# Attention followed by a two-layer MLP in split fp16: a planner that knows of the port shared by VectorE and GpSimd, lo halves in two operations, and new tables

## The chip, the core and the metric

The kernel is one program on one core of a Trainium2 chip. The time is that of the device from the program's start to its end, in microseconds (us). Names of engines are those of the profile: PE is TensorE, PEld its weight loads, DVE is VectorE, ACT is ScalarE, POOL is GpSimd, and SP issues the DMAs.

## What is computed

```
scores = q @ k.T / sqrt(64)                    # 4 batches, 12 heads, 448 rows, head size 64
scores = where(upper triangle, -1e9, scores)
attn = softmax(scores)
x = (attn @ v)  -> (4 * 448, 768)
h = x @ w_in                                   # w_in 768 x 2048
g = h - tanh(h)
out = g @ w_out                                # w_out 2048 x 768
```

The two weight matrices arrive as 64-bit floats and are turned into 32-bit ones on the core. q, k and v arrive as 32-bit floats.

## The kernel before

**Precision.** All large products run in fp16 with each operand split in two: hi is the scaled value rounded to fp16, lo is the scaled value minus hi. A product is three matmuls (hi·hi, hi·lo, lo·hi). `split` makes the halves. `scaled` makes hi on DVE, ACT or POOL. The lo half is either one DVE pass (`scalar_tensor_tensor`: multiply, then subtract) or, on POOL, two passes: scale the source in place, then subtract hi.

**Stages.** `w_in_chunk` (8 times) turns 256 columns of w_in into fp32, measures their size with a matmul against ones, and splits them; `w_out_half` (twice) does the same for w_out. `first_rows` computes attention for the first 128 rows of two batches at a time; the first pair of batches makes chunk c, the second pair chunk c2. `attention(b)` computes the other 320 rows of batch b, in six pairs of heads: `prep` splits k, q and v, `weights_unit` and `weights_last` do scores, softmax and the split of the weights, a DMA transposes the weights, and `values` multiplies them with v. `mlp_g` is the first MLP layer for a chunk (16 column blocks of 18 matmuls each, evacuated by a tanh on ACT and a pass on DVE, and then split into g), `mlp2` the second layer, whose result leaves through the tile `o`.

**What sets the order.** Nothing is issued where it is written. Every operation is recorded in `Work` with a rank, and `schedule` then plays a list schedule: each engine takes, of what is ready, the operation of lowest rank, with a cost per operation from `cost`. The instructions are issued in the order that this gives, and each engine keeps that order on the chip. Two tables feed it. `CFG` says for each kind of operation on which engine its instances go in turn (V, A, G for DVE, ACT, POOL): `"p": "VAVV"` puts the hi halves of the softmax weights on DVE, ACT, DVE, DVE and so on. `RANK` sets the ranks of the stages; matmuls of the MLP have a rank of 10 and more, attention(b) for b of 1 and more has `RANK["att"] + 10 + b - 1` plus a sixth per pair.

**The shared port in the plan.** `schedule` keeps a time `port` until which operations marked `shared` of DVE and POOL exclude each other. An operation of POOL is marked when it reads a tile. One of DVE is marked when it reads two large operands from SBUF, or when it is a `tensor_scalar` with one large input, no other input, and equal types of input and output.

Of the kernel before, what the change touches and what calls it, by code (L numbers as in the profile page):

```python
# [15 lines left out]
AF = mybir.ActivationFunctionType  # L16
ALU = mybir.AluOpType
# [8 lines left out]
class Work:  # L26
# [43 lines left out]
    def add(self, eng, method, args, kw):  # L70
# [26 lines left out]
        if eng == "G":  # L97
            shared = bool(ins)
        else:
            two_ports = method == "tensor_scalar" and len(big) == 1 and outs[0].dtype == big[0].dtype and len(ins) == 1  # L100
            shared = eng == "V" and (len(big) > 1 or two_ports)
# [4 lines left out]

    def either(self, tag, *ways):
# [6 lines left out]
        n = self.turn[tag] = self.turn.get(tag, -1) + 1  # L114
        way = CFG[tag]
        self.ops[-1].update(eng=way[n % len(way)], tag=(tag, n))

    def cost(self, eng, method, outs, ins):
# [18 lines left out]
        if eng == "A":  # L137
            return n * 0.833 + (51 if psum else 94) + 93 * aps + 93 * (len(outs) > 1), 0.0
        if eng == "G":
            if method == "tensor_tensor":  # L140
                return n * 1.885 + 148, 0.0
            return n * 0.83 + 245, 0.0
# [16 lines left out]
    def schedule(self):  # L159
        n = len(self.ops)  # L160
# [14 lines left out]
        for _ in range(n):  # L175
# [5 lines left out]
            o = self.ops[i]  # L181
            if e in o["shared"] and port > t:
# [19 lines left out]
            if e in o["shared"]:  # L202
                t = max(t, port)
                port = t + o["cost"]
            o["start"] = t
# [13 lines left out]
            for j in users[i]:  # L219
                left[j] -= 1  # L220
                f = self.ops[j]["eng"]
                at[j] = max(at[j], end + (self.SAME if f == e else self.LAT)[f])
                if not left[j]:
                    heapq.heappush(waiting[f], (at[j], j))
# [34 lines left out]
def attention_then_mlp(ctx, tc, qk, v, w_in, w_out, out):  # L259
# [565 lines left out]

CFG = {"early": 4, "e_bufs": 4, "b_out": "A", "b_qk": "AAV", "shift_in": "AGG", "inverse": "A", "w_in": "AVGA", "w_in_lo": "GGV", "shift_out": "AVAG", "w_out": "VAAA", "w_out_lo": "V", "p0": "G", "p0t": "AVAA", "x0": "VVVAAV", "g0": "GGGA", "g0_lo": "V", "g2": "GVVV", "g2_lo": "G", "g": "VVGV", "g_lo": "G", "o": "V", "k_first": "VAVGGA", "k_first_lo": "VVGV", "q_first": "G", "q_first_lo": "V", "v_first": "GVA", "v_first_lo": "V", "p_first": "AGGAVA", "p_first_lo": "V", "k": "GVGG", "k_lo": "V", "q": "VA", "q_lo": "G", "v": "GVAV", "v_lo": "GVV", "p": "VAVV", "p_lo": "VGV", "x": "AAVA"}
RANK = {"c0": -14.292, "w_in": -12.778, "evac": 4.208, "w_out": 7.476, "c0b": 9.316, "att0": -13.314, "att": -0.165}

# [29 lines left out]
```

## Time and profile before

| what | us |
|---|---|
| median of 3 runs (lowest, highest) | 605.71 (604.11, 606.19) |
| profiled execution, its own time | 603.75 |
| its span, first to last instruction | 602.0 |
| PE busy | 559.2 |
| DVE busy | 451.6 |
| POOL busy | 312.9 |
| ACT busy | 294.8 |

A PE that the profile shows as busy is one with a matmul under way; a matmul of 384 columns is shown for 326 ns, while the next one starts 163 ns later. So waiting of PE is read from gaps, and the pace from the starts. DVE instructions overlap a little in the same way, by some 75 ns. All instructions carry the line of one helper (L232), so groups are told apart by their tiles.

### The profile page before, as it was taken

How to read it: one execution, taken by the hardware profiler on the slowest of the kernel's cores; microseconds unless marked ns; L12 is line 12 of the kernel's file. 1: busy time of each engine (PE TensorE's matmuls, PEld its weight loads, DVE VectorE, ACT ScalarE, POOL GpSimd, SP SyncE). 2: the span in 40 equal slices, each digit the busy share in tenths (PEclk: the TensorE clock that was granted, in tenths of full speed). 3: DMA queues.
4: the chain of work that ended last, by engine and by line, in shares of the span. 5: the costliest groups of instructions: out<-in, count | busy, mean ns of one | idle time of the engine just before them, and what ended most of it. 6: DMA issues, size and time to landing. Idle time of an engine off the chain costs nothing.

```text
span 602.0 us, 13635 instructions
## 1 busy us (share of the span) xinstructions
PE 559.2 (93%) x5144; PEld 375.9 (62%) x5144; DVE 451.6 (75%) x1286; ACT 294.8 (49%) x796; POOL 312.9 (52%) x389
## 2 busy tenths in 40 slices
PE   3688689999999999999999999999999999999997
PEld 3456468876555556765666666665666566776664
DVE  3889997989999999999959999921999961332000
ACT  5899899983366755553436463400644430121000
POOL 3577962883232157886528788510687820465000
PEclk9999899999999999999999999999999999999999
DMA  8995467645386974448563556640334281000100
GB/s 283 327 337 186 141 196 212 188 127 222 95 164 142 181 164 79 80 99 181 119 141 72 106 123 174 128 74 27 84 60 79 42 146 43 13 2 1 27 27 26
DMA packets 113378, 74.02 MB, mean 123 GB/s; under 512 B 89760, under 2 KB 99488, under 8 KB 112800
## 3 DMA queue, kind: packets, MB, share of 16 engines
q1 hardware_dynamic: 113312, 73.15, 48.8%
q8 instruction: 40, 0.66, 0.5%
q14 instruction: 26, 0.21, 0.1%
HBM read 45.61 MB, written 5.51 MB: 85 GB/s over the span
## 4 chain that ended last, share of the span: by engine, by line
PE 31%; DVE 31%; issue 3%; DMA 3%; POOL 3%; ACT 1%; DVEq 0%; SPq 0%; POOLq 0%; ACTq 0%
PE b_m L232 29%; DVE pn L232 6%; DVE prob L232 6%; DVE small L232 5%; DVE first L232 3%; DVE t L232 3%; DVE g L232 2%; PE b_x L232 2%; DVE v L232 2%; DVE k L232 1%; DMA e<-in_v_dram 1%; DVE x L232 1%; DMA slot<-in_qk_dram 1%; POOL g L232 1%; DMA pt<-pn 1%
## 5 line engine op out<-in xcount | busy, mean ns | idle before, releaser
L232 PE MATMUL b_m<-x,w_in 128*128 128x320 f16 (+1 forms) x1728 | 230.1, 291 | 15.3 <-DVE t L232 14.2
L232 PEld LDWEIGHTS <-w_in 128*128 128x128 f16 x1728 | 167.5, 98 | 72.1 <-issue 22.9
L232 PE MATMUL b_m<-slot,g 128*128 128x384 f16 x1152 | 192.4, 326 | 0.0
L232 PEld LDWEIGHTS <-g 128*128 128x128 f16 x1152 | 110.7, 98 | 74.9 <-issue 3.9
L232 ACT ACTIVATE prob<-prob,small 128x256 f32<-128x256 f32 (+2 forms) x102 | 58.8, 577 | 70.0 <-DVE small L232 69.5
L232 POOL TENSOR_SCALAR t<-t,small 128x320 f32<-128x320 f32 (+1 forms) x80 | 53.4, 668 | 51.6 <-DVE g L232 43.9
L232 ACT ACTIVATE t<-b_m,small 128x320 f32<-128x320 f32 (+1 forms) x96 | 48.1, 502 | 63.7 <-PE b_m L232 53.6
L232 DVE SCALAR_TENSOR_TENSOR t<-b_m,small,t 128x320 f32<-128x320 f32 (+1 forms) x96 | 49.9, 520 | 30.2 <-ACT t L232 30.0
L232 DVE TENSOR_SCALAR o<-b_m,small 128x384 f32<-128x384 f32 x28 | 17.1, 610 | 70.3 <-PE b_m L232 70.2
L232 POOL TENSOR_TENSOR g<-t,g 128x320 f16<-128x320 f32 x64 | 54.2, 847 | 5.3
L232 DVE CUSTOM_DVE_ANT_0 prob<-b_s,mask,small 128x384 f32<-128x384 f32 (+1 forms) x87 | 46.1, 545 | 0.2
L232 DVE SCALAR_TENSOR_TENSOR slot<-b_s,e 128x384 int32<-128x384 int32 x64 | 34.6, 547 | 5.5 <-ACT b_s L232 3.2
L232 DVE SCALAR_TENSOR_TENSOR pn<-prob,small,pn 128x256 f16<-128x256 f32 (+2 forms) x60 | 37.5, 645 | 0.1
L232 PEld LDWEIGHTS <-v 128*64 128x64 f16 x1296 | 31.5, 111 | 8.2 <-issue 8.0
L232 PE MATMUL b_m<-slot,first 128*128 128x384 f16 x192 | 33.6, 326 | 0.0
L232 PEld LDWEIGHTS <-first 128*128 128x128 f16 (+2 forms) x282 | 21.7, 98 | 17.6 <-issue 6.2
L232 PE MATMUL b_s<-k,q 64*128 64x256 f16 (+2 forms) x342 | 30.7, 317 | 0.4 <-DVE small L232 0.3
L232 ACT ACTIVATE e<-slot 128x768 f32<-128x768 f32 (+1 forms) x30 | 26.3, 876 | 5.4 <-DMA slot<-in_moe_w_in_dram 3.5
L232 POOL TENSOR_SCALAR prob<-prob,small 128x384 f32<-128x384 f32 (+2 forms) x24 | 15.4, 640 | 24.5 <-DVE pn L232 16.3
L232 DVE TENSOR_SCALAR g<-t,small 128x320 f16<-128x320 f32 x48 | 27.1, 564 | 0.4
L232 PE MATMUL b_x<-pt,v 128*64 128x64 f16 (+1 forms) x1026 | 26.3, 207 | 0.3 <-DMA pt<-pn 0.3
L232 DVE TENSOR_SCALAR small<-small 128x1 f32<-128x1 f32 (+4 forms) x159 | 26.0, 178 | 0.2
(137 smaller groups left out, 815.9 us busy)
## 6 DMA issues: line engine op xcount, KB each, us to landing
slot<-in_moe_w_in_dram SPq DMA_DIRECT2D x16, 768.0 KB, 6.2
slot<-in_qk_dram SPq DMA_DIRECT2D x18, 384.0 KB, 3.3
slot<-in_moe_w_out_dram SPq DMA_DIRECT2D x8, 768.0 KB, 4.7
e<-in_moe_w_out_dram SPq DMA_DIRECT2D x8, 768.0 KB, 4.5
e<-in_v_dram SPq DMA_DIRECT2D x3, 1536.0 KB, 6.6
out_dram<-o SPq DMA_DIRECT2D x24, 192.0 KB, 1.9
first<-in_qk_dram SPq DMA_DIRECT2D x6, 384.0 KB, 3.4
g<-in_qk_dram SPq DMA_DIRECT2D x6, 256.0 KB, 6.5
```

What stands on the lines that cost most here:

```text
L232: getattr(self.eng[o["eng"]], method)(*args, **kw)
```

## The change

The planner: a DVE `tensor_scalar` with one large input counts as shared whenever neither its input nor its output lies in PSUM, whatever the types and the scale operand. That takes in the hi halves, which go from fp32 to fp16 with a scale per row. A shared operation may now start a little ahead of the port's release (`lead`) and holds it a little longer. POOL's two-input cost rises by 20, some ACT costs by 75. An operation of cost zero adds no delay to its user on the same engine.

The lo half: `split` records two operations. The first scales the source in place, on POOL or on ACT, or does nothing when DVE does the lo half in one pass. The second is the DVE pass or POOL's subtraction. The letter A in a lo table now means: ACT scales, POOL subtracts.

The tables: most entries of `CFG` and all of `RANK` are new.

```diff
-            two_ports = method == "tensor_scalar" and len(big) == 1 and outs[0].dtype == big[0].dtype and len(ins) == 1
+            two_ports = method == "tensor_scalar" and len(big) == 1 and not any(x.space == bass.MemoryType.PSUM for x in outs + ins)
...
+    def nothing(self, eng):
+        self.ops[-1]["alts"][eng] = [], [0.0]
+        self.ops[-1].setdefault("shared", set())
...
-            return n * 0.833 + (51 if psum else 94) + 93 * aps + 93 * (len(outs) > 1), 0.0
+            words = ins[0].space != bass.MemoryType.PSUM and (o.space == bass.MemoryType.PSUM or ins[0].ap[-1][0] > 1)
+            return n * 0.833 + (51 if psum else 94) + 93 * aps + 93 * (len(outs) > 1) + 75 * (words and not aps), 0.0
...
+            lead = 190.0 if e == "V" else 135.0
+            if e in o["shared"] and port - lead > t:
...
-                t = max(t, port)
-                port = t + o["cost"]
+                t = max(t, port - lead)
+                port = t + o["cost"] + (75.0 if e == "V" else 22.0)
...
-        def lo_pool():
-            G.tensor_scalar(src, src, s, 1.0, ALU.mult, ALU.mult)
-            G.tensor_tensor(lo, src, hi, ALU.subtract)
-        wk.either(tag + "_lo", lambda: V.scalar_tensor_tensor(lo, src, s, hi, ALU.mult, ALU.subtract), lo_pool)
+        wk.either(tag + "_lo", lambda: wk.nothing("V"), lambda: G.tensor_scalar(src, src, s, 1.0, ALU.mult, ALU.mult),
+                  lambda: A.activation(src, src, AF.Copy, scale=s))
+        wk.either(tag + "_lo", lambda: V.scalar_tensor_tensor(lo, src, s, hi, ALU.mult, ALU.subtract),
+                  lambda: G.tensor_tensor(lo, src, hi, ALU.subtract), again=True, A="G")
...
-RANK = {"c0": -14.292, "w_in": -12.778, "evac": 4.208, "w_out": 7.476, "c0b": 9.316, "att0": -13.314, "att": -0.165}
+RANK = {"c0": -25.732, "w_in": -23.993, "evac": 0.14, "w_out": 7.706, "c0b": -9.849, "att0": -0.222, "att": -8.619}
```

What the new table does to the splits, counted in the two programs. Each cell is the number of instructions on DVE / ACT / POOL; POOL's two passes of a lo half count as two, and an ACT scaling with its POOL subtraction as one on each.

| operation | before | after |
|---|---|---|
| w_in hi | 2 / 4 / 2 | 0 / 0 / 8 |
| w_in lo | 2 / 0 / 12 | 8 / 0 / 0 |
| w_out lo | 16 / 0 / 0 | 12 / 4 / 4 |
| g lo of chunk c | 16 / 0 / 0 | 0 / 0 / 32 |
| softmax weights hi, batches 1 to 3 | 67 / 23 / 0 | 45 / 45 / 0 |
| softmax weights lo, batches 1 to 3 | 60 / 0 / 60 | 23 / 45 / 89 |
| k hi, batches 1 to 3 | 5 / 0 / 13 | 6 / 6 / 6 |
| k lo, batches 1 to 3 | 18 / 0 / 0 | 4 / 5 / 23 |
| q hi, batches 1 to 3 | 9 / 9 / 0 | 18 / 0 / 0 |
| q lo, batches 1 to 3 | 0 / 0 / 36 | 6 / 6 / 18 |
| v hi, batches 1 to 3 | 9 / 4 / 5 | 0 / 13 / 5 |
| v lo, batches 1 to 3 | 12 / 0 / 12 | 0 / 0 / 36 |
| g hi, the last four chunks | 48 / 0 / 16 | 32 / 32 / 0 |
| g lo, the last four chunks | 0 / 0 / 128 | 32 / 0 / 64 |
| o | 28 / 0 / 0 | 7 / 21 / 0 |

The order at three places follows.

POOL while w_in is prepared (slot_69 and slot_70 hold the fp32 chunk, w_in_76 and following its halves, pn_103 softmax rows of `first_rows`, e_74 the low words of the next chunk). Before:

```order
L232 TENSOR_SCALAR slot_69<-slot_69,small_105 128x1536
L232 TENSOR_TENSOR w_in_76<-slot_69,w_in_76 128x1536
L232 TENSOR_SCALAR e_74<-slot_68 128x768
L232 TENSOR_SCALAR slot_70<-slot_70,small_105 128x1536
L232 TENSOR_TENSOR w_in_77<-slot_70,w_in_77 128x1536
L232 TENSOR_TENSOR pn_103<-pn_103,small_105 128x512
```

and now:

```order
L239 TENSOR_SCALAR w_in_76<-slot_69,small_105 128x1536
L239 TENSOR_TENSOR pn_103<-pn_103,small_105 128x512
L239 TENSOR_SCALAR w_in_77<-slot_70,small_105 128x1536
L239 TENSOR_SCALAR e_74<-slot_67 128x768
L239 TENSOR_TENSOR pn_103<-pn_103,small_105 128x512
L239 TENSOR_SCALAR w_in_78<-slot_69,small_105 128x1536
```

The scaling in place and the subtraction of the lo half are gone from POOL, which makes the hi half instead; the lo half is a `SCALAR_TENSOR_TENSOR` of 1536 columns in DVE's queue.

POOL in the attention of a later batch (prob_99 and following hold the softmax rows, pn_103 and first_91 the split weights or k and q, t_86 and following MLP rows, g_84 their split). Before:

```order
L232 TENSOR_SCALAR t_87<-t_87,small_105 128x320
L232 TENSOR_TENSOR g_84<-t_87,g_84 128x320
L232 TENSOR_SCALAR t_88<-t_88,small_105 128x320
L232 TENSOR_TENSOR g_84<-t_88,g_84 128x320
L232 TENSOR_SCALAR prob_99<-prob_99,small_105 128x256
L232 TENSOR_TENSOR pn_103<-prob_99,pn_103 128x256
```

and now:

```order
L239 TENSOR_SCALAR prob_99<-prob_99,small_105 128x256
L239 TENSOR_SCALAR slot_70<-slot_70,small_105 128x448
L239 TENSOR_TENSOR pn_103<-prob_99,pn_103 128x256
L239 TENSOR_TENSOR pn_103<-prob_100,pn_103 128x256
L239 TENSOR_TENSOR pn_103<-prob_102,pn_103 128x384
L239 TENSOR_TENSOR first_91<-slot_70,first_91 128x448
L239 TENSOR_TENSOR first_91<-slot_70,first_91 128x320
```

POOL's queue holds lo halves of softmax weights, k and q where it held those of g; several are subtractions alone, whose scaling stands in ACT's queue.

DVE behind the last split of softmax weights of the last batch (pn_103 written from prob_102 or first_91; x_85 is the attention's result on its way to the MLP, o_89 and o_90 results of the MLP, t and g the evacuation of the MLP's first layer). Before:

```order
L232 TENSOR_SCALAR pn_103<-prob_102,small_105 128x448
L232 SCALAR_TENSOR_TENSOR pn_103<-first_91,small_105,pn_103 128x448
L232 SCALAR_TENSOR_TENSOR x_85<-b_x_110,x_85 128x320
L232 TENSOR_SCALAR o_90<-b_m_112,small_105 128x384
L232 TENSOR_SCALAR x_85<-b_x_110 128x320
L232 SCALAR_TENSOR_TENSOR x_85<-b_x_110,x_85 128x320 x2
L232 TENSOR_SCALAR o_89<-b_m_111,small_105 128x384
L232 TENSOR_SCALAR o_90<-b_m_112,small_105 128x384
L232 SCALAR_TENSOR_TENSOR t_88<-b_m_111,small_105,t_88 128x320
```

and now:

```order
L239 SCALAR_TENSOR_TENSOR pn_103<-prob_102,small_105,pn_103 128x448
L239 TENSOR_SCALAR o_90<-b_m_112,small_105 128x384
L239 TENSOR_SCALAR small_105<-small_105 128x2
L239 COPY small_105<-small_105 64x2
L239 SCALAR_TENSOR_TENSOR t_87<-b_m_111,small_105,t_87 128x320
L239 SCALAR_TENSOR_TENSOR g_84<-t_87,small_105,g_84 128x320
L239 SCALAR_TENSOR_TENSOR t_88<-b_m_112,small_105,t_88 128x320
```

Behind that split stood the evacuations of one chunk's first layer (16 of t), now those of two (32). On PE, behind the last score matmul, stood 288 matmuls of 320 columns and 432 of 384; now 576 and 630, and one more pair's values.

## Rows read from the trace of the kernel before

**Rows 1.** The page's busy times by engine (us, share of the span, instructions), and its 40 slices of 15 us for PE and DVE, each digit a busy share in tenths.

```profile
PE 559.2 (93%) x5144; PEld 375.9 (62%) x5144; DVE 451.6 (75%) x1286; ACT 294.8 (49%) x796; POOL 312.9 (52%) x389
...
PE   3688689999999999999999999999999999999997
...
DVE  3889997989999999999959999921999961332000
```

**Rows 2.** Stretches of 20 us: length, then busy us (and instructions) of PE, PEld, DVE, ACT and POOL, the granted clock, the DMA engines' share and GB/s.

```profile
60.00:80.00 20.00, 12.59 (x106) 9.91 (x104) 18.80 (x66) 17.77 (x41) 15.82 (x13) 0.91 0.44 138
...
80.00:100.00 20.00, 18.89 (x174) 15.43 (x172) 17.52 (x49) 19.67 (x51) 11.40 (x13) 1.00 0.75 213
...
340.00:360.00 20.00, 18.55 (x234) 12.93 (x233) 20.00 (x56) 12.19 (x38) 16.67 (x22) 1.00 0.60 123
...
380.00:400.00 20.00, 20.00 (x170) 12.37 (x168) 11.08 (x27) 4.53 (x13) 7.28 (x9) 1.00 0.78 140
400.00:420.00 20.00, 20.00 (x171) 12.38 (x169) 3.39 (x6) 0.95 (x2) 1.85 (x2) 1.00 0.06 20
...
460.00:480.00 20.00, 18.20 (x133) 11.32 (x131) 19.13 (x48) 9.06 (x26) 15.03 (x19) 1.00 0.28 54
```

**Rows 3.** The same for three longer stretches.

```profile
160.00:500.00 340.00, 331.64 (x3438) 212.78 (x3438) 296.01 (x831) 159.59 (x480) 193.48 (x254) 1.00 0.54 112
106.00:136.00 30.00, 27.97 (x249) 24.19 (x249) 27.77 (x55) 25.37 (x52) 25.39 (x33) 1.00 0.53 156
136.00:160.00 24.00, 23.12 (x148) 14.11 (x147) 22.50 (x39) 8.27 (x14) 6.16 (x9) 1.00 0.47 179
```

**Rows 4.** What PE waited for from 106 us to the end: us in total, times, the longest.

```profile
PE b_m L232 <- DVE t L232: 6.9, 12, 1.0
PE b_s L232 <- DVE small L232: 1.5, 3, 1.0
PE b_scales L232 <- DVE small L232: 1.2, 2, 0.9
```

**Rows 5.** Timeline (start us, us, instructions): PE at two long runs of one shape, and the last lines of the chain that ended last.

```profile
503.55 8.95 PE L232 MATMUL b_m<-slot,g 128*128 128x384 f16 x54
512.33 7.91 PE L232 MATMUL b_m<-x,w_in 128*128 128x320 f16 x57
...
503.62 94.82 PE b_m L232 x630
598.46 0.62 DVE o L232
```

**Rows 6.** Timeline of the preparation of w_in: the size matmuls on PE of the first, the fifth and the last chunk, POOL's lo half of the last chunk, and the first evacuation-bound start of chunk c2.

```profile
19.40 1.46 PE L232 MATMUL b_scales<-w_in,ones 128*128 128x256 bf16 x6
...
49.32 0.82 PE L232 MATMUL b_scales<-w_in,ones 128*128 128x256 bf16 x6
...
72.63 1.48 PE L232 MATMUL b_scales<-w_in,ones 128*128 128x256 bf16 x6
...
79.56 1.57 POOL L232 TENSOR_SCALAR slot<-slot,small 128x1536 f32<-128x1536 f32 x1 [0.46 <-ACT w_in L232]
81.21 3.12 POOL L232 TENSOR_TENSOR w_in<-slot,w_in 128x1536 f16<-128x1536 f32 x1
...
106.21 12.13 PE L232 MATMUL b_m<-x,w_in 128*128 128x256 f16 x108 [0.38 <-DVE t L232]
```

**Rows 7.** The passes that write one tile (duration in ns: least / median / most, first and last start in us, shapes): w_in, softmax weights, k and g.

```profile
L232 DVE SCALAR_TENSOR_TENSOR w_in<-slot,small,w_in x2: 1819/1954/2090, 41.6 to 65.5; 128x1536 f16<-128x1536 f32 x2
L232 DVE TENSOR_SCALAR w_in<-slot,small x2: 1280/1293/1306, 28.5 to 63.8; 128x1536 f16<-128x1536 f32 x2
L232 POOL TENSOR_SCALAR w_in<-slot,small x2: 1547/1548/1548, 40.0 to 69.7; 128x1536 f16<-128x1536 f32 x2
L232 DVE SCALAR_TENSOR_TENSOR pn<-prob,small,pn x60: 461/604/1309, 166.0 to 482.4; 128x256 f16<-128x256 f32 x24, 128x384 f16<-128x384 f32 x24, 128x448 f16<-128x448 f32 x12
L232 DVE TENSOR_SCALAR pn<-prob,small x41: 333/431/1240, 170.3 to 489.2; 128x384 f16<-128x384 f32 x16, 128x256 f16<-128x256 f32 x15, 128x448 f16<-128x448 f32 x10
L232 DVE SCALAR_TENSOR_TENSOR k<-slot,small,k x14: 659/778/1210, 160.4 to 457.8; 128x448 f16<-128x448 f32 x14
L232 DVE SCALAR_TENSOR_TENSOR v<-e,small,v x12: 734/740/1302, 210.1 to 465.8; 128x512 f16<-128x512 f32 x12
L232 POOL TENSOR_TENSOR pn<-prob,pn x15: 669/914/1283, 225.6 to 490.5; 128x256 f16<-128x256 f32 x6, 128x384 f16<-128x384 f32 x6, 128x448 f16<-128x448 f32 x3
L232 DVE TENSOR_SCALAR g<-t,small x48: 371/427/1005, 231.2 to 552.9; 128x320 f16<-128x320 f32 x48
L232 DVE SCALAR_TENSOR_TENSOR g<-t,small,g x16: 457/480/1645, 59.5 to 104.8; 128x256 f16<-128x256 f32 x16
```

**Rows 8.** Timeline of DVE and POOL where a hi half of g on DVE meets a lo half of v on POOL.

```profile
231.17 0.37 DVE L232 TENSOR_SCALAR g<-t,small 128x320 f16<-128x320 f32 x1
...
232.18 1.16 POOL L232 TENSOR_TENSOR v<-e,v 128x512 f16<-128x512 f32 x1
...
232.52 1.00 DVE L232 TENSOR_SCALAR g<-t,small 128x320 f16<-128x320 f32 x1
```

**Rows 9.** Groups of DVE from 160 to 500 us: busy us, mean ns of one, idle us before them.

```profile
L232 DVE TENSOR_SCALAR g<-t,small 128x320 f16<-128x320 f32 x36 | 22.4, 623 | 0.0
```

More of the change, by code (lines that the diff above doesn't have):

```diff
@@ L105, in add, with either @@
         op["move"] += move
-    def either(self, tag, *ways):
+    def either(self, tag, *ways, again=False, A="A"):
         self.ops.append(dict(alts={}, deps=set(), rank=self.rank, move=0.0))
@@ L113, in either @@
         self.alt = None
-        n = self.turn[tag] = self.turn.get(tag, -1) + 1
-        way = CFG[tag]
-        self.ops[-1].update(eng=way[n % len(way)], tag=(tag, n))
+        n = self.turn[tag] = self.turn.get(tag, -1) + (not again)
+        way = CFG[tag].replace("A", A)
+        self.ops[-1].update(eng=way[n % len(way)], tag=(tag, n), A=A)
+    def nothing(self, eng):
+        self.ops[-1]["alts"][eng] = [], [0.0]
+        self.ops[-1].setdefault("shared", set())
     def cost(self, eng, method, outs, ins):
@@ L137, in cost @@
         if eng == "A":
-            return n * 0.833 + (51 if psum else 94) + 93 * aps + 93 * (len(outs) > 1), 0.0
+            words = ins[0].space != bass.MemoryType.PSUM and (o.space == bass.MemoryType.PSUM or ins[0].ap[-1][0] > 1)
+            return n * 0.833 + (51 if psum else 94) + 93 * aps + 93 * (len(outs) > 1) + 75 * (words and not aps), 0.0
         if eng == "G":
             if method == "tensor_tensor":
-                return n * 1.885 + 148, 0.0
+                return n * 1.885 + 168, 0.0
             return n * 0.83 + 245, 0.0
@@ L181, in schedule @@
             o = self.ops[i]
-            if e in o["shared"] and port > t:
+            lead = 190.0 if e == "V" else 135.0
+            if e in o["shared"] and port - lead > t:
                 other = [x for x in ready[e] if e not in self.ops[x[1]]["shared"]]
@@ L221, in schedule @@
                 f = self.ops[j]["eng"]
-                at[j] = max(at[j], end + (self.SAME if f == e else self.LAT)[f])
+                at[j] = max(at[j], end + (self.LAT[f] if f != e else self.SAME[f] if o["cost"] else 0.0))
                 if not left[j]:
@@ L823, in attention_then_mlp @@
         wk.emit()
-CFG = {"early": 4, "e_bufs": 4, "b_out": "A", "b_qk": "AAV", "shift_in": "AGG", "inverse": "A", "w_in": "AVGA", "w_in_lo": "GGV", "shift_out": "AVAG", "w_out": "VAAA", "w_out_lo": "V", "p0": "G", "p0t": "AVAA", "x0": "VVVAAV", "g0": "GGGA", "g0_lo": "V", "g2": "GVVV", "g2_lo": "G", "g": "VVGV", "g_lo": "G", "o": "V", "k_first": "VAVGGA", "k_first_lo": "VVGV", "q_first": "G", "q_first_lo": "V", "v_first": "GVA", "v_first_lo": "V", "p_first": "AGGAVA", "p_first_lo": "V", "k": "GVGG", "k_lo": "V", "q": "VA", "q_lo": "G", "v": "GVAV", "v_lo": "GVV", "p": "VAVV", "p_lo": "VGV", "x": "AAVA"}
-RANK = {"c0": -14.292, "w_in": -12.778, "evac": 4.208, "w_out": 7.476, "c0b": 9.316, "att0": -13.314, "att": -0.165}
+CFG = {"early": 4, "e_bufs": 4, "b_out": "A", "b_qk": "AVA", "shift_in": "VGAGAA", "inverse": "VAVV", "w_in": "G", "w_in_lo": "V", "shift_out": "GAGVVV", "w_out": "GAA", "w_out_lo": "AVVV", "p0": "G", "p0t": "VA", "x0": "A", "g0": "AGGG", "g0_lo": "G", "g2": "AAGG", "g2_lo": "GVG", "g": "AAVV", "g_lo": "VG", "o": "AVAA", "k_first": "AVAA", "k_first_lo": "GV", "q_first": "GVV", "q_first_lo": "VGVA", "v_first": "AAVV", "v_first_lo": "GVAA", "p_first": "GA", "p_first_lo": "V", "k": "GAV", "k_lo": "AGVG", "q": "V", "q_lo": "GGAAVV", "v": "AGAA", "v_lo": "G", "p": "AVVA", "p_lo": "VAGA", "x": "VA"}
+RANK = {"c0": -25.732, "w_in": -23.993, "evac": 0.14, "w_out": 7.706, "c0b": -9.849, "att0": -0.222, "att": -8.619}
 _OUTS = [((1792, 768), "float32")]
```

## The prediction

> **What bounds the kernel now.** I read the page first: PE is busy 93% of the span, no other engine over 75%, and PE's slices are full from the tenth on [rows 1]. So the time is PE's work plus what PE loses, and only losses can be won back. Then PE's pace. In a run of 54 matmuls of 384 columns the starts are (8.95 - 0.33) / 53 = 0.163 us apart, in one of 57 of 320 columns (7.91 - 0.30) / 56 = 0.136 us [rows 5]. At the end 630 of them run for 94.82 us without a wait, and 3.6 us follow for the last output [rows 5]. The change leaves every matmul in place, so it can't touch that pace.
>
> Where PE loses shows in the stretches. Up to 106 us, where chunk c2 starts, PE is fed by everything else; from 60 to 80 us it is busy 12.59 of 20 us while DVE is at 18.80, ACT at 17.77 and POOL at 15.82 [rows 2]. No single engine is full there. From 106 us on PE is idle 2.0 us to 136, 0.9 us to 160 and 8.4 us to 500 [rows 3], together 11.3, and none after. Almost all of that is put down to DVE: 6.9 us in the wait for the pass that empties a bank of the MLP's first layer, 2.7 us for small DVE results [rows 4]. They fall where DVE is full: 18.55 us of PE beside 20.00 of DVE from 340 us, 18.20 beside 19.13 from 460 [rows 2]. From 380 to 420 us it is the other way round: PE full, DVE busy 14.5 of 40 us [rows 2].
>
> DVE's fullness is partly waiting. A hi half of g of 320 columns takes 0.37 us alone [rows 8]; the one that starts at 232.52, while POOL subtracts, ends at 233.52, just after POOL's end at 233.34 [rows 8]. Between 160 and 500 us the 36 of them have a mean of 623 ns against a least of 371 [rows 7, 9]: 9 us lost in this group alone. These are the passes that the old plan did not count as excluding POOL.
>
> **The change, part by part.** The planner's code runs before the launch and costs nothing on the chip; it acts through order and tables.
>
> *Start, up to 106 us.* The splits of w_in leave POOL and go to DVE. Removed from DVE are two lo and two hi halves, 2 x 1.95 + 2 x 1.29 = 6.5 us; added are eight lo halves, 8 x 1.95 = 15.6 us [rows 7]. Of the 16 lo halves of g of chunk c, 0.48 us each [rows 7], nearly all ran on DVE before 106 us and now run on POOL; but several of them lay behind what PE waits for, so I count half, 4 us, as relief. DVE's bill at the start is thus about +9 - 4 = +5 us, and 5 us is the upper bound if DVE sets the start. The other bound comes from the chain of one chunk of w_in. On POOL a lo half costs 1.57 + 3.12 = 4.7 us [rows 6], on DVE 1.95; the hi half stays near 1.5 us. Six of eight chunks become 2.7 us shorter, with two chunks in work at a time: 6 x 2.7 / 2 = 8 us. The size matmuls run from 19.40 to 72.63 us for eight chunks [rows 6], 7.6 us a chunk, so this chain may be the pace: then -8. As neither DVE (18.80) nor POOL (15.82) is full from 60 to 80 us [rows 2], neither end holds by itself. I take -1, near the middle, and keep -8 and +5.
>
> *Middle, 106 us to the last score.* In batches 1 to 3 DVE loses 37 lo halves of weights at about 0.53 us of engine time (the median of 0.604 less the overlap of 75 ns), 22 hi halves at 0.33, 14 lo halves of k at 0.60, 12 of v at 0.66 and 9 hi halves of v at about 0.40 (no row of it alone; the hi halves of weights start at 0.333) [rows 7]. That is 19.6 + 7.3 + 8.4 + 7.9 + 3.6 = 46.8 us. It gains 9 hi halves and 6 lo halves of q (nearest rows again the halves of weights: 3 + 3 us), and small things, scalings of the row sums and a few halves of x, for which I allow 5. Net -36 us. Results `o` give another -8, since most go to ACT, at 0.6 us each behind PE [rows 5]. ACT (159.59 of 340 us) and POOL (193.48) have the room [rows 3].
>
> But the new order also takes PE's work away from this stretch. Behind the last score stand 288 more matmuls of 320 columns, 198 more of 384 and one more pair's values (54 matmuls, about 1.4 us): 39.2 + 32.2 + 1.4 = 73 us of PE that used to cover DVE. Chunk 2's evacuation and halves, about 11 us of DVE, go with it. So in place of 296 us of DVE in 340 us (0.87) [rows 3] I expect 296 - 36 - 8 - 11 + 5 (halves of g that come to DVE) = 246 us in 340 - 73 = 267 us: 0.92, if the stalls at the port stay. Those I estimate at 0.15 us a pass, between 0.25 for the hi halves of g (0.623 less 0.371) and 0.12 for the lo halves of k (median less least) [rows 7, 9]; DVE has about 270 passes that share the port in this stretch (60 a batch of 1 to 3, about as many in batch 0, and g), so 40 us. By the table they fall to 34 a batch, in all to 180, and at the same 0.15 us 14 us of stalls go with them: 232 of 267, 0.87. Compare it with the DVE-bound part of before: without the 40 us from 380 on, 281.5 us in 300, 0.94. So DVE comes out less tight where it was tight, by 2 to 7 points. I take two thirds of the 11.3 us as won back: -7.5, with 0 and -11 as bounds.
>
> *End.* The run without waits grows from 95 to some 160 us. There PE's pace holds, as at present [rows 5]; per column block DVE has about 1 us of passes in 18 x 0.136 = 2.4 us. Zero.
>
> *Sum.* 603.75 us for the profiled execution - 1 - 7.5 = 595.2. That execution lies 2 us below the median of the three runs, and the change is applied to the median: 605.71 - 8.5 = 597.2 us.
>
> **What speaks against it.** The trace shows that DVE and POOL hold each other up [rows 8], and this change moves lo halves from DVE to POOL, whose subtraction alone takes 0.914 us in the median where DVE's whole lo half takes 0.604 [rows 7]. The Trainium skill, in Perfetto Trace Analysis, section "Optimizing Scalar/DVE Operations", warns of just this: the two share an SBUF read port, "so offloading operations between those two might not help". The trace agrees on the mechanism (1.00 us in place of 0.37), and whether the moved work pays is what no row of before shows.
>
> **Rivals.**
> - *The start is paced by the chain of w_in.* Then -8 instead of -1: 605.7 - 8 - 7.5 = 590.2. For it: 7.6 us a chunk, and POOL's lo half of the last chunk ends only at 84.3 us [rows 6]. Against: DVE gets busier there. Chance 0.18.
> - *Half and half.* Only a third of the waits goes (-3.7) and DVE sets the start (+5): 607.0, hardly to be told from no change. Chance 0.15.
> - *The port gives back what it takes.* Each lo half moved to POOL holds up a DVE pass for as long as it saved; the waits of 11.3 us stay, and the start costs +3 to +5: 608.7 to 610.7. The point from which it decides: DVE has 267 - 206 = 61 us to spare over its unstalled work (246 less 40), over 180 shared passes, so a mean stall over 0.3 us a pass fills DVE altogether; the hi halves of g now stand at 0.25. This is the mechanism that the skill's sentence names. Chance 0.17.
> - *POOL's longer chain holds up the weights.* A lo half is now a pass on ACT, then a subtraction in POOL's queue, behind other batches' lo halves; the transposing DMA and the `values` matmuls wait for it, and in a shorter stretch fewer MLP matmuls stand in between. If twelve of these transposes came 1 us late for PE: 605.7 + 12 - 1 = 617. Against: POOL is busy only 57% from 160 to 500 us [rows 3]. Chance 0.08.
>
> **How the numbers follow.** The forecast, 597.2 us, has a chance of 0.42; its own range is 592 to 603.8. With the first rival (0.18) that makes 0.60 for faster by over 0.3%, which is about what a measurement of this kernel can tell from no change (603.9 to 607.5). Half and half (0.15) and the mild edge of the third rival (0.03) make 0.18 for the same; the rest of the third (0.14) and the fourth (0.08) make 0.22 for slower. The range runs from 587, the first rival with all waits gone, to 611, the port rival's end; it leaves out the fourth rival and a part of what lies below the first, some 0.15 together.
>
> **What the profile after would show.** Start: c2's first long run of 256-column matmuls begins near 105 us (98 if the w_in chain was the pace, 111 if DVE is), and the eight size matmuls lie closer than 7.6 us apart. Middle: PE's waits for `t` from DVE after that point sum to under 4 us; the hi halves of g on DVE have a mean under 0.5 us. End: a run of some 160 us without waits of PE. Wrong: a mean of DVE's shared passes above 0.3 us over their least, PE waiting for `values` on a DMA of weights, or a start of c2 after 112 us.

## The result, and the profile after

| | before | after |
|---|---|---|
| median of 6 runs each, us (lowest, highest) | 604.74 (604.11, 606.19) | 610.05 (607.35, 610.56) |
| profiled execution's span | 602.0 | 608.7 |
| PE busy | 559.2 | 559.5 |
| DVE busy | 451.6 | 421.5 |
| POOL busy | 312.9 | 325.3 |
| ACT busy | 294.8 | 353.5 |

The ratio is 1.008, with a 95% interval of 1.006 to 1.010: slower by 0.8%, where 1.4% faster was forecast. DVE did lose 30 us of busy time, and the end gained nothing by it.

The page of the changed kernel, busy times and slices, beside [rows 1]:

```profile
PE 559.5 (92%) x5144; PEld 375.5 (62%) x5144; DVE 421.5 (69%) x1229; ACT 353.5 (58%) x885; POOL 325.3 (53%) x400
...
PE   3468898899999999998999999999999999999997
...
DVE  4899985977899999999999999997024400343000
```

DVE is full in one piece from 167 to 411 us, where it used to have a hole at 380 [rows 1, 2], and then nearly idle; the load has moved forward as the order said. In windows of 20 us and in the whole stretch up to the last score (columns as in [rows 2, 3]):

```profile
280.00:300.00 20.00, 18.13 (x168) 11.05 (x167) 20.00 (x61) 11.29 (x27) 16.54 (x20) 1.00 0.40 91
...
380.00:400.00 20.00, 17.58 (x211) 10.81 (x210) 19.93 (x56) 14.73 (x39) 17.41 (x21) 1.00 0.52 89
440.00:460.00 20.00, 20.00 (x142) 13.69 (x141) 5.65 (x12) 4.18 (x8) 2.65 (x4) 1.00 0.05 17
...
138.00:418.00 280.00, 267.30 (x2859) 167.95 (x2860) 263.68 (x764) 199.19 (x524) 203.09 (x246) 1.00 0.65 136
```

PE loses where DVE stands at 20 of 20 us, 2.4 us in the window at 380. From 440 us on it loses nothing. The start (timeline of PE: first and last size matmuls of w_in, the wait at chunk c2, the first matmuls of the second layer; [rows 6] has the first three of before, where the second layer started at 136.49):

```profile
17.42 1.44 PE L239 MATMUL b_scales<-w_in,ones 128*128 128x256 bf16 x6 [1.38 <-ACT w_in L239]
...
68.05 0.82 PE L239 MATMUL b_scales<-w_in,ones 128*128 128x256 bf16 x6
...
105.29 0.81 PE L239 MATMUL b_m<-x,w_in 128*128 128x256 f16 x6 [1.52 <-DVE t L239]
...
138.74 1.46 PE L239 MATMUL b_m<-slot,g 128*128 128x384 f16 x8
```

The chunks of w_in lie (68.05 - 17.42) / 7 = 7.2 us apart instead of 7.6, and c2 starts at 105.3 instead of 106.2. By the second layer 2.2 us are lost, and 4.5 us more from there to the end (470.0 instead of 465.5 us). The first number means little. Three of the runs below (`before, POOL's lo halves as one filling`, `before, DVE's lo halves moved`, `before, hi halves of g on ACT`) issue the same instructions as before in the same order on every engine up to 210 us, and their second layers begin at 137.3, 138.1 and 138.2 us; two others do as after up to 210 us, and begin it at 137.1 and 137.9. So the start alone scatters by 1.6 to 1.7 us among these executions. From there to the last score PE is idle for 9.0 us before and for 12.7 after: that is where the two differ. What PE waited for from 138 us on (`t` from 136 us on before, then after; [rows 4] starts at 106 us):

```profile
PE b_m L232 <- DVE t L232: 4.7, 8, 1.0
...
PE b_s L239 <- DVE small L239: 4.6, 6, 2.1
PE b_scales L239 <- DVE small L239: 4.1, 6, 1.5
PE b_m L239 <- DVE t L239: 1.4, 3, 0.8
PE b_x L239 <- DVE x L239: 1.3, 3, 0.5
```

The waits haven't gone, they have changed their owner. The bank evacuations (`t`) hold up PE little; the small DVE results do, the scales and row sums on which the next scores and size matmuls wait: 8.7 us, 2.7 before. So the passes on `small` are the place to look. All DVE passes that scale one small tile into another from 140 to 482 us, first of before, then of after (count: least/median/most ns, first and last start, shapes):

```profile
L232 DVE TENSOR_SCALAR small<-small x96: 127/162/660, 154.2 to 468.1; 128x1 f32<-128x1 f32 x32, 128x2 f32<-128x2 f32 x28, 128x2 int32<-128x2 int32 x24, 128x8 f32<-128x8 f32 x8
```

```profile
L239 DVE TENSOR_SCALAR small<-small x143: 124/174/1180, 152.6 to 446.9; 128x2 f32<-128x2 f32 x71, 128x1 f32<-128x1 f32 x36, 128x2 int32<-128x2 int32 x24, 128x8 f32<-128x8 f32 x8
```

A pass over two columns does 124 ns of work and takes up to 1.18 us. The groups of the two-column ones to the last score show where the time is (busy us, mean ns, idle before), before and after:

```profile
L232 DVE TENSOR_SCALAR small<-small 128x2 f32<-128x2 f32 x28 | 5.1, 184 | 0.0
```

```profile
L239 DVE TENSOR_SCALAR small<-small 128x2 f32<-128x2 f32 x68 | 20.6, 312 | 1.5 <-ACT prob L239 1.2
L239 DVE RECIPROCAL small<-small 128x2 f32<-128x2 f32 x78 | 11.8, 156 | 0.5
L239 DVE TENSOR_SCALAR small<-small 128x2 int32<-128x2 int32 x24 | 8.2, 342 | 0.1
L239 DVE TENSOR_SCALAR small<-small 128x1 f32<-128x1 f32 x36 | 6.5, 182 | 0.0
```

40 of the 68 are new on DVE: `inverse`, the scaling of the softmax sums, had gone to ACT by the old table ("A") and goes to DVE by the new one ("VAVV"). Here two columns wait, one column and reciprocals don't. One such place, first DVE, then POOL:

```profile
285.92 1.09 DVE L239 TENSOR_SCALAR small<-small 128x2 f32<-128x2 f32 x4
...
285.46 0.79 POOL L239 TENSOR_TENSOR g<-t,g 128x320 f16<-128x320 f32 x1
286.24 0.69 POOL L239 TENSOR_SCALAR e<-e,small 128x512 f32<-128x512 f32 x1
```

Four small passes take 1.09 us while POOL subtracts and scales; PE waits 0.42 us for their result at 287.39.

**An account of DVE.** For each kernel I split the time from 140 us to the last score in three: idle is what no DVE instruction covers; held is, over all passes that touch no PSUM bank, their time above the 15th percentile of passes of the same operation and shape in the two kernels (and above a further 15 ns); work is the rest. A pass is said to meet the POOL instruction with which it overlaps longest.

| kernel | stretch, us | work | held | idle |
|---|---|---|---|---|
| before | 342.6 | 264.5 | 41.2 | 36.9 |
| after | 278.0 | 214.9 | 47.2 | 15.9 |

Work fell by 49.6 us, held time rose by 6.0: that of large passes fell from 38.5 to 31.2 us, that of small ones rose from 2.7 to 16.0. Held time lies where POOL runs: large passes that meet no POOL instruction are held 0.0 us (49 after), those that meet a subtraction 0.35 us each (73 of 180; before 0.31, 85 of 271), and small scalings that meet one 0.28 us (44 of 140, 12.3 us in all; before 11 of 96, 0.2 us).

### The profile page after: what moved, and what is told of

It is laid out like the page before. It is cut to its first block, busy times and chain, and to the rows that moved or that the text cites. A ratio compares the mean times of both kernels' runs of the same rounds, so it can differ in the third digit from the quotient of the medians.

```text
span 608.7 us, 13743 instructions
## 1 busy us (share of the span) xinstructions
PE 559.5 (92%) x5144; PEld 375.5 (62%) x5144; DVE 421.5 (69%) x1229; ACT 353.5 (58%) x885; POOL 325.3 (53%) x400
## 5 line engine op out<-in xcount | busy, mean ns | idle before, releaser
L239 POOL TENSOR_SCALAR t<-t,small 128x320 f32<-128x320 f32 (+1 forms) x59 | 34.5, 587 | 127.9 <-ACT g L239 89.1
L239 ACT ACTIVATE prob<-prob,small 128x384 f32<-128x384 f32 (+2 forms) x138 | 77.8, 568 | 29.5 <-DVE small L239 28.8
L239 ACT ACTIVATE o<-b_m,small 128x384 f32<-128x384 f32 x21 | 12.1, 575 | 78.6 <-PE b_m L239 78.6
L239 DVE TENSOR_SCALAR o<-b_m,small 128x384 f32<-128x384 f32 x7 | 4.3, 609 | 77.1 <-PE b_m L239 77.1
L239 DVE TENSOR_SCALAR small<-small 128x1 f32<-128x1 f32 (+5 forms) x215 | 48.6, 243 | 3.0 <-ACT prob L239 1.2
L239 POOL TENSOR_TENSOR g<-t,g 128x320 f16<-128x320 f32 (+1 forms) x48 | 38.0, 794 | 2.5
L239 DVE SCALAR_TENSOR_TENSOR pn<-prob,small,pn 128x256 f16<-128x256 f32 (+2 forms) x44 | 29.8, 698 | 2.8 <-ACT pn L239 1.7
L239 PEld LDWEIGHTS <-first 128*128 128x128 f16 (+2 forms) x282 | 21.8, 98 | 15.4 <-issue 3.6
L239 ACT ACTIVATE g<-t,small 128x320 f16<-128x320 f32 (+1 forms) x36 | 19.9, 553 | 16.6 <-DVE t L239 16.4
L239 POOL TENSOR_TENSOR pn<-prob,pn 128x384 f16<-128x384 f32 (+2 forms) x31 | 27.7, 906 | 3.3 <-ACT prob L239 2.9
L239 ACT ACTIVATE b_s<-slot 128x384 f32<-128x384 f32 x48 | 24.3, 514 | 7.3 <-DVE slot L239 2.6
```

The lines of the kernel that those rows point to most:

```text
L239: getattr(self.eng[o["eng"]], method)(*args, **kw)
```

## The experiments

Every ratio is to the kernel before, run beside it on the same chip (605.74 us with the first four, 605.34 with the next, 605.21 with the last). Unless something else is said, the edits are in the loop that issues the instructions, so that the order stays as it was. The main theories: S, the held small passes cost the time; R, GpSimd's reads for the moved lo halves cost it; L, GpSimd's longer chain makes the halves late; O, the order counts more than what goes where; N, any other order would move the time as much. Other letters are explained where they stand.

| run | median us | ratio (95%) |
|---|---|---|
| after, `inverse` on ACT | 611.82 | 1.010 (1.008, 1.012) |
| before, `inverse` on DVE | 614.40 | 1.013 (1.011, 1.016) |
| after, POOL's lo halves as one filling | 602.78 | 0.995 (0.994, 0.997) |
| after with the old tables | 617.20 | 1.019 (1.016, 1.022) |
| after with the old planner | 634.26 | 1.049 (1.046, 1.051) |
| after, POOL's lo halves as two fillings | 599.62 | 0.991 (0.989, 0.992) |
| before, POOL's lo halves as one filling | 597.35 | 0.987 (0.985, 0.989) |
| before, DVE's lo halves moved | 634.94 | 1.049 (1.047, 1.051) |
| after, single columns | 605.33 | 1.000 (0.998, 1.001) |
| before, hi halves of g on ACT | 601.24 | 0.994 (0.992, 0.996) |
| after, another order | 608.60 | 1.006 (1.004, 1.007) |
| before, another order | 608.11 | 1.004 (1.003, 1.006) |

**`inverse` back on ACT, and `inverse` on DVE in the kernel before.**

```diff
+            eng = o["eng"]
+            if o.get("tag", ("",))[0] == "inverse":
+                eng = "A"
...
```

(In the kernel before it is "V" in three of four cases, as in the new table.)

> The changed kernel in its own order, but the scaling of the row sums (`inverse`, two columns) always on ACT, as before. Theory S (these small DVE passes are held at the port by POOL's lo halves: the 2-column DVE passes of 160 to 430 us lose some 14 us to stalls after the change, 1 us before): the stalls of the small passes fall under 5 us and the time falls by 4 to 6 us, to a ratio of 0.998 to 1.002 against the kernel before. Theory L (the moved lo halves themselves and the smaller PE cover cost the time, the small passes only wait where DVE would wait anyway): the time stays, 1.006 to 1.010.

> The kernel before in its own order, with three of four of those small scalings on DVE in place of ACT. Theory S: 2-column passes of DVE stall by 6 to 10 us more and the time rises by 3 to 6 us, to 1.005 to 1.010. Theory L: 0.999 to 1.003.

The first gave nothing (611.8; theory L's range, theory S had 4 to 6 us less), the second cost 9 us (theory S had 3 to 6). Moving the passes away from DVE lowers held time only from 47.2 to 43.6 us, since the other two-column passes stay, and DVE now waits for ACT: of the reciprocals that follow, with what ended their idle time,

```profile
L242 DVE RECIPROCAL small<-small 128x2 f32<-128x2 f32 x78 | 12.1, 159 | 8.0 <-ACT small L242 7.5
```

So the first run doesn't tell whether held small passes cost time; it trades one wait for another. Of the 12.1 us that the second's span is longer, 5.8 lie in the start (its second layer begins at 142.30 us). There `inverse` has four columns, and one such pass on DVE ran beside POOL's subtraction for a lo half of w_in, to its end (DVE, then POOL; the pass is 2.91 of the 2.96 us, where others of its shape take 0.16):

```profile
58.11 2.96 DVE L235 TENSOR_SCALAR small<-small 128x4 f32<-128x4 f32 x2
...
57.90 3.10 POOL L235 TENSOR_TENSOR w_in<-slot,w_in 128x1536 f16<-128x1536 f32 x1
```

Four of these nine passes are held, 3.9 us in all. What else the start lost isn't settled: it scatters by 1.7 us by itself, and the granted clock from 60 to 80 us was 0.66 there and 0.91 before, a longer part of it at the lower level (1.2 GHz). The other 6.3 us go along with the two-column passes: in 140 to 494 us the small ones are held 9.9 us, 2.7 before.

**What POOL's subtractions cost by reading.** In batches 1 to 3 the lo halves of k, q, v and weights that POOL makes are filled with zeros, once or twice, so that these runs leave the lo halves out. A filling reads nothing; it also needn't wait for what the subtraction reads, such as a half that ACT scales.

```diff
+                if eng == "G" and method == "tensor_tensor" and o.get("tag", ("",))[0] in ("k_lo", "q_lo", "v_lo", "p_lo"):
+                    self.nc.gpsimd.memset(args[0], 0.0)
+                    continue
```

> The changed kernel in its own order, but POOL's subtractions for the lo halves of k, q, v and the softmax weights in batches 1 to 3 write zeros instead, so those halves are left out of the result; POOL's queue, its waits and the order stay, but these instructions read nothing and are shorter. If POOL's reads at the shared port are what fills DVE: DVE's stalls between 160 and 430 us fall from about 48 to under 25 us and the time to 0.985 to 0.998. If the new order and the smaller PE cover are the cause: DVE's stalls may fall, the time stays within 1.004 to 1.010.

> The changed kernel in its order; in batches 1 to 3 each subtraction of GpSimd that makes a lo half of k, q, v or the weights is replaced by two fillings of that half with zeros, so the lo halves are left zero. The run with one filling took 602.8 us, but GpSimd was also busy 0.5 us less for each. With two, GpSimd's time is nearly that of the subtraction (at 512 columns 2 x 0.52 = 1.04 against 1.22 us), and it still reads nothing. Theory R (the reads hold up VectorE): 602 to 605 us, as with one filling, and stalls of VectorE's shared passes near 22 us from 160 to 440 us. Theory L (GpSimd's longer chain makes the halves late, whatever it reads): 608 to 611 us.

> The kernel before in its order, with the same edit: the subtractions of GpSimd that make lo halves of k, q, v and weights in batches 1 to 3 are replaced by one filling with zeros each (these lo halves are left zero). It has about half as many of them as the changed kernel. Theory R: the gain goes with their number, about half of the 7 us that the edit gave in the changed kernel: 601 to 603 us. If the reads of the halves that were moved aren't what distinguishes the kernels: a gain of 6 us or more here too, 600 us or less. Theory L: no gain beyond 1 us, 604 to 606 us.

With two fillings POOL is nearly as busy as with subtractions (185.5 of 268.4 us in the stretch, 201.2 of 278.0 after), and the gain isn't smaller but larger, 10 us, more than either theory had: that POOL is busy for long is not what costs (so far theory L falls; whether halves that wait for ACT's scaling come late isn't tested, as the fillings drop that wait). Held time falls from 47.2 to 34.6, and PE's idle time from the second layer to the last score from 12.7 to 6.2. But one filling gives 8.0 us in the kernel before, with half as many subtractions, where it gives 7.3 after, and held time falls by 12.4 us in both. So theory R falls as the reason for the *difference*: the halves that POOL made already cost as much as all of them now; the moved ones added no price of their own that shows. The small passes keep most of their held time, 16.0 us after, 13.4 with one filling and 15.4 with two.

The run with one filling also shows which passes POOL holds up by writing. DVE, then POOL, in two places:

```profile
334.20 0.62 DVE L243 SCALAR_TENSOR_TENSOR pn<-prob,small,pn 128x384 f16<-128x384 f32 x1 [0.16 <-ACT pn L243]
...
385.30 2.71 DVE L243 TENSOR_SCALAR q<-slot,small 128x320 f16<-128x320 f32 x1
...
334.23 0.42 POOL L241 MEMSET pn<- 128x384 f16 x1
...
385.10 0.71 POOL L243 TENSOR_SCALAR prob<-prob,small 128x384 f32<-128x384 f32 x1
385.76 0.52 POOL L241 MEMSET v<- 128x512 f16 x1
386.22 0.78 POOL L241 MEMSET first<- 128x384 f16 x2
386.94 0.47 POOL L241 MEMSET pn<- 128x448 f16 x1
387.36 0.47 POOL L241 MEMSET k<- 128x448 f16 x1
```

A lo half with two inputs runs through a filling at its normal length. A hi half (0.36 us alone) ends 0.18 us after the last of six POOL instructions in a row.

**Rules and tables apart.** The first run has the new planner with the tables of before, the second the new tables and the two-part lo half with the planner's costs and port rules of before; both orders are new. Of the edits, `CFG` of the first and the costs and the mark of the second go back in the same way.

```diff
-RANK = {"c0": -25.732, "w_in": -23.993, "evac": 0.14, "w_out": 7.706, "c0b": -9.849, "att0": -0.222, "att": -8.619}
+RANK = {"c0": -14.292, "w_in": -12.778, "evac": 4.208, "w_out": 7.476, "c0b": 9.316, "att0": -13.314, "att": -0.165}
```

```diff
-            lead = 190.0 if e == "V" else 135.0
+            lead = 0.0
...
-                port = t + o["cost"] + (75.0 if e == "V" else 22.0)
+                port = t + o["cost"]
```

> The changed planner with the tables of before. If the tables carry the loss and the planner's new rules alone are harmless or good: 0.995 to 1.002. If the rules' order costs: 1.004 or more.

> The changed kernel's split of the lo halves and its two tables, but the planner's costs and its rules of the port as before the change. Counterpart of the run with the new rules and the old tables (617.2 us). Theory R (what the change loses, it loses because the lo halves that were moved to GpSimd read SBUF and hold up VectorE; the order matters less): 608 to 613 us, as the same operations go to the same engines. Theory O (the order that the planner makes is what counts, and rules and tables fit only together): another mismatch, 614 us or more.

617.2 and 634.3: worse than either kernel. The same operations on the same engines cost 24 us more in the order of the old rules, so theory O holds: rules and tables fit only together, and neither can be judged alone.

**The move of the lo halves alone**, in the order of before.

```diff
+            moved = eng == "V" and o.get("tag", ("",))[0] in ("k_lo", "q_lo", "v_lo", "p_lo")
+            if moved:
+                eng = "G"
...
+                if moved and method == "tensor_scalar":
+                    self.nc.scalar.activation(args[0], args[1], AF.Copy, scale=args[2])
...
```

> The kernel before in its order, with the move of the lo halves alone: in batches 1 to 3 each lo half of k, v and the weights that VectorE made in one pass (63 of them) is made as in the changed kernel, the scaling on ScalarE and the subtraction on GpSimd. VectorE loses about 63 x 0.55 = 35 us of work. Theory R (the port gives back what it takes): no gain, 605 to 612 us, and VectorE's shared passes are held up longer each than the 0.15 us of before. The forecast's theory (the relief is real and only the new order spoils it): 600 us or less. A loss above 614 us would mean late halves (theory L): waits of TensorE for weights or values.

It cost 29.6 us, which only theory L allowed for. The account shows where: work 226.8 us (38 less), held 49.0 (8 more), idle 96.0 (59 more). DVE now waits. What it waited for from 138 to 500 us (us in total, times, longest), and its timeline at one of these places:

```profile
DVE t L239 <- ACT t L239: 12.4, 15, 3.0
...
DVE small L239 <- ACT small L239: 9.9, 9, 3.5
...
DVE prob L239 <- POOL pn L239: 8.7, 9, 1.9
DVE prob L239 <- POOL first L239: 7.2, 4, 2.7
```

```profile
251.39 0.62 DVE L239 CUSTOM_DVE_ANT_0 prob<-b_s,mask,small 128x384 f32<-128x384 f32 x1 [1.55 <-POOL first L239]
```

The next scores can't be written until POOL has read the old ones out of `prob`, behind its queue: 15.9 us in the last two lines. That is theory L's mechanism, met by DVE more than, as expected, by TensorE, whose waits for a DMA of weights are 2.6 us. ACT, which took over the scalings, makes DVE wait for longer still: the first two lines are 22.3 us, 1.0 and 2.1 in the kernel before. In the new order DVE stands idle for 15.9 us only.

**Single columns.** Each two-column scaling of small tiles on DVE is made as two passes of one column.

```diff
+                if o["eng"] == "V" and method == "tensor_scalar" and args[0].shape == args[1].shape and tuple(args[0].shape) == (P, 2):
+                    for c in (0, 1):
+                        getattr(self.eng["V"], method)(args[0][:, c:c + 1], args[1][:, c:c + 1], *args[2:], **kw)
+                    continue
```

> The changed kernel in its order; each two-column scaling of VectorE on small tiles (two inputs of one column each would be the same numbers) is made as two passes of one column. In the changed kernel from 140 to 418 us the two-column ones (68 of f32, 24 of int32) are held up 15 us in all by GpSimd, the one-column ones (36) hardly (0.03 us each). The second pass adds about 0.1 us of VectorE's time, some 10 us in all. Theory S (these holds, which the forecast had not counted, are real time lost on VectorE's queue): VectorE comes out about 5 us shorter, 604 to 608 us. If the hold only passes on to VectorE's next pass that shares the port: nothing is saved, the 10 us of added passes show, 611 to 616 us.

605.33 us: 4.7 less than after, inside theory S's range, and equal to before. The order is the same on every engine, and the first pass that is split comes at 134.6 us. The passes that were split, as tile group, and the place shown above:

```profile
L241 DVE TENSOR_SCALAR small<-small x190: 96/142/214, 157.8 to 442.8; 128x1 f32<-128x1 f32 x142, 128x1 int32<-128x1 int32 x48
```

```profile
284.52 0.45 DVE L241 TENSOR_SCALAR small<-small 128x1 f32<-128x1 f32 x6
284.88 0.16 DVE L243 TENSOR_SCALAR small<-small 128x8 f32<-128x8 f32 x1
```

The longest is 214 ns instead of 1180; six passes and an eight-column one take 0.52 us where four took 1.09. Held time falls by 13.6 us to 33.6, work rises by 4.9. Hardly anything is passed on to the next large pass: these are held 30.4 us, before the edit 31.2. The traces show less of the gain than the medians. Of the 4.0 us between the two spans 2.1 lie ahead of the second layer (136.6 instead of 138.7 us), where the edit changes next to nothing and the start scatters by nearly as much; 1.9 us lie behind it, and PE's idle time from there to the last score is 11.9 us instead of 12.7. The clock doesn't explain the start: from 40 to 60 us it was granted at 0.79 after (a part of the time at the lower level, 1.2 GHz) and at 1.00 here, but also at 0.80 in the other order of after (below), whose second layer begins at 136.2 us. The kernel before with single columns was not run; its small passes are held 2.7 us, so that by the account there is little to win.

**Relief by ACT.** In the order of before, hi halves of g leave DVE for ACT.

```diff
+            eng = "A" if o.get("tag", ("",))[0] == "g" and o["eng"] == "V" else o["eng"]
...
```

> The kernel before in its order; the hi halves of g that VectorE makes from the second chunk group on (48, at 0.37 us alone and 0.25 us held up each) are made by ScalarE, at about 0.45 us. The counterpart of the run that moved the lo halves to ScalarE and GpSimd (634.9 us): here the same engine is relieved, of 23 us, by an engine that VectorE doesn't wait for at a port, and in one operation. Theory D (VectorE's work with its holds sets what TensorE loses; relief pays if it brings no new holds and no second queue): 596 to 601 us. Theory Q (any operation taken out of an order that was planned for its engine comes late): 606 us or more.

601.24 us, just above theory D's range, and faster than both kernels. The group of [rows 9] is now on ACT, and PE's largest wait from 106 us on is 4.3 us (6.9 in [rows 4]):

```profile
L233 ACT ACTIVATE g<-t,small 128x320 f16<-128x320 f32 x36 | 20.0, 555 | 16.9 <-DVE t L233 16.5
```

```profile
PE b_m L233 <- DVE t L233: 4.3, 8, 1.1
```

The moved passes were 11.1 us of work and 8.6 us of held time; the account falls by 7.1 and 3.1. Other work has slid into the stretch, and of the held time more than half comes back: other passes are held 5.5 us more, 3.2 of it on small ones.

**How far another order alone moves the time.**

```diff
-                port = t + o["cost"] + (75.0 if e == "V" else 22.0)
+                port = t + o["cost"] + (70.0 if e == "V" else 22.0)
```

(In the kernel before, the 70 in `n * 0.52 + 70` of `cost` became 72.)

> A control: the changed kernel with one cost in the planner 75 ns changed to 70 ns. The same operations go to the same engines, and about 1260 of 3099 places of the order differ; the planner's own sum moves by 0.7 us. If the change's loss of 0.8% is a property of what goes where, this gives 608 to 612 us. If one order among many equals makes several us of difference (theory N), it can land anywhere from 603 to 620 us, and a 5 us difference between two plans says little of the change.

> The same control for the kernel before: one cost of the planner, 70 ns for a pass of VectorE, set to 72 ns; 1365 of 2787 places of the order differ, the planner's own sum moves by 3 us. Without theory N: 603 to 608 us. With it: anywhere from 600 to 618 us.

608.60 (1.5 below after) and 608.11 (3 above before). The second lies just outside the range without theory N, so a part of the theory holds: in these two tries a change of order without any other reason was worth 1.5 and 3 us; more tries could show more. That is more than half of the change's 5 us, and PE's idle time from the second layer to the last score shows it too: 9.0 us before, 11.5 in its other order, 12.7 after and in its other order. The other order of after is also a warning about the account: it has more held time (52.1 us, 20.2 of it on small passes) and yet is 1.5 us faster. Held time is not time lost one for one.

## Why the prediction was wrong, step by step

*What bounds the kernel.* Right. PE's busy time and its run at the end are as before; the difference is in what PE loses, most of it to DVE.

*Start, -1 us.* The step itself held: c2 at 105.3 (105 forecast), chunks 7.2 us apart (less than 7.6), so neither bound came, though at the scatter of the start a microsecond can't be told from nothing. The +2.2 us at the second layer are hardly more than that scatter, and the other order of after begins it at 136.2 us; no run shows them to belong to the change.

*Middle, DVE's work.* Right: -36 - 8 - 11 + 5 = -50 us, measured -49.6. So close a match is luck, as the two stretches differ a little and some terms were allowances. The shorter stretch was right in kind: 64.6 us shorter (342.6 to 278.0), where 73 were forecast. The counts of large passes were right too, 271 and 180 for 270 and 180.

*Middle, held time.* **This is the step that failed**: "at the same 0.15 us 14 us of stalls go with them". They rose by 6 us, from 41.2 to 47.2, an error of 20 us on an engine that was to have 35 us to spare: 13 us are small passes (2.7 to 16.0 us), which the sum left out, and 7 are large ones, which fell by 7.3 us where 14 were forecast. Three things were wrong in it. It counted large passes only; 12.3 us of the held time after is of small ones that meet a subtraction, 0.2 before, and the `inverse` passes that the new table brings to DVE were entered as work and not as sharers of the port. It took the stall per pass as fixed; it is 0.31 to 0.35 us for a large pass that meets a subtraction, and the share of large passes that do rose from 85 of 271 to 73 of 180, as POOL's busy share of the stretch rose from 0.57 (193.9 of 342.6 us) to 0.72 (201.2 of 278.0). And fewer passes don't mean fewer stalls: of the 91 by which large passes became fewer, only 12 are ones that meet a subtraction; 40 met nothing and 39 a scaling of POOL, which holds less (0.10 to 0.13 us). The run with single columns takes 13.6 us of held time away without moving an operation, and by the medians the change's loss is gone. "The mean of g's hi halves under 0.5 us" fails in the same way: from 138 to 440 us the 16 on DVE stand at 612 ns, hardly below [rows 9].

*Middle, waits won back, -7.5.* It was to follow from that step, and fell with it. The wait for `t` from 106 us on fell under 4 us as forecast, barely (6.9 to 3.9), but waits for `small` took its place.

*End, zero.* Right. The end of the chain that ended last, beside [rows 5]:

```profile
489.96 115.29 PE b_m L239 x756
605.25 0.02 issue
605.28 0.58 ACT o L239
```

*Rivals.* "The port gives back what it takes" has the time, 608.7 to 610.7 for 610.05, and the kind of cause, but not the mechanism in detail, so that the hit on the time is partly luck. Its turning point, 0.3 us per large shared pass, wasn't reached (31.2 us over 180, 0.17), and lo halves moved to POOL don't cost more than those already there, as the fillings show in both kernels. What was given back came in good part through small passes, which the forecast didn't count as sharers. The planner did: in its test a tile is large from two columns on (`x.size() > x.shape[0]`), so that both kernels' planners mark the two-column scalings as shared and single columns as not. The order that came of it didn't keep them apart from POOL on the chip. The Trainium skill, Perfetto Trace Analysis, section "Optimizing Scalar/DVE Operations", warns that offloading between the two engines might not help; the trace agrees, with 49.6 us less work on DVE in the stretch and 5 us lost, and the run with ACT as the helper (0.994) is the other half of its advice. "POOL's longer chain" didn't come in the new order (PE's waits for a DMA of weights are 0.5 us), but has a part in the loss of the old one (634.9 us). The w_in chain and half and half didn't decide.

How much is shown? Making the two-column passes single, with all else as it was, takes back 4.7 of the 5 us in the medians; of these the two traces place only 1.9 us where the edit acts. Against that stand the 1.5 to 3 us that another order makes, and the order with more held time and less time. So the held small passes are shown to cost time, and the exact share of the loss is not. Why DVE's lighter load after that repair is worth nothing against before is argued only: work and held time fill 253.4 of 274.1 us (0.92), where the forecast had 0.87. That share alone doesn't sort the runs: with the old tables it is 0.87, at 617.2 us. Not tried: single columns in the kernel before, and an order planned for single columns.

## What to carry to other kernels

When passes of one engine share something with another engine, price them by how many will meet the other at work, not by a mean per pass; take the passes off and the rest meets the other more often. Look at the spread (least, median, most) of the smallest instructions too: here two columns of work cost up to 1.18 us, and making them one column at a time paid for twice as many instructions. When a full engine is to be relieved, try first an engine that shares nothing with it (hi halves of g on ACT gained 4 us; `inverse` on ACT, on whose result DVE waits, gained nothing), and plan the order for it, since a like move in the old order cost 5%. Before a part of the time is explained, see how much it differs between executions of the same instructions: here the start alone differs by 1.7 us.

## What the runs showed of the hardware

- A DVE `tensor_scalar` from SBUF to SBUF is held beside POOL at two columns as at 320 (up to 1.18 us after), and at four (2.91 us with `inverse` on DVE in the kernel before); at one column it isn't (96 to 214 ns in 190 passes with single columns). Reciprocals of two columns weren't held after (138 to 167 ns in 81); in the run with one filling one of 81 took 748 ns, beside three fillings in a row. The Trainium skill, SBUF — State Buffer, section "Who interferes with whom", has it that a DVE pass in a two-port mode is blocked for the whole of POOL's instruction; the pass of 1.18 us agrees: it starts at 211.88 us and ends 0.03 us after a subtraction of 1.15 us. That two columns are enough for it shows only in the runs.
- A held pass can be passed over by several POOL instructions in a row: 2.71 us through six of them.
- POOL's fillings, which read nothing, hold up `tensor_scalar` passes (in the run with one filling 0.58 us in the mean over the 13 large ones whose longest overlap is with one, 0.42 over 19 small ones) and not those with two inputs (0.01 over 10). The same section says that two inputs contend with POOL's reads only; the runs agree.
